# Top-32 attention with a feed-forward block behind it: when SyncE writes and reads the turned weights, and where POOL combines the output weights

## The chip, the cores and the metric

The kernel runs on one core of one Trainium2 chip. A core has five engines that work side by side, each through its own instructions in order: PE (matrix products; PEld is its loading of the stationary operand), DVE and ACT and POOL (element-wise work), and SP (SyncE, which here only issues transfers, DMAs). An engine waits on semaphores for the others. PE writes to PSUM, a small memory in banks; everything else lies in SBUF, with 128 partitions, or in DRAM.

The metric is the time of one execution on the device, in microseconds (us): the median of the runs.

## The reference

```python
def _attn_ref(q, k, v):                       # (8, 8, 576, 64) each
    top_k, scale = 32, 1.0 / np.sqrt(D)
    scores = scale * np.matmul(q, k.transpose(0, 1, 3, 2))
    kth = np.partition(scores, -top_k, axis=-1)[..., -top_k:-top_k + 1]
    scores = np.where(scores >= kth, scores, -1000000000.0)
    scores = scores - np.max(scores, axis=-1, keepdims=True)
    attn = np.exp(scores)
    attn = attn / (np.sum(attn, axis=-1, keepdims=True) + 1e-09)
    return np.matmul(attn, v).astype(np.float32)

def _moe_ref(x, w_in, w_out):                 # x: (4608, 512), w_in: (512, 2048)
    h = x @ w_in
    g = h - np.tanh(h)
    return (g @ w_out).astype(np.float32)
```

The attention's output, with the heads side by side, is the x of the second block. The output is 4608 x 512 in float32.

## The kernel before

**Steps.** A step is one query tile of 128 rows for a pair of heads, and there are 144: for each of the 8 batches four full tiles for each of four pairs of heads, and two steps for the 64 rows that remain. A step goes through several passes of the loop in `run` (L973). In pass n, DVE searches step n for the 32 largest scores of each row (`search`, from L340). Meanwhile POOL and ACT make the mask of step n-1 (`mask`, L386) and its exponentials (`expo`, L428). Between the rounds of the search of step n, ACT divides the weights of step n-2 (`divide`, L453), and at the end of that search DVE turns them in blocks of 32 x 32 into the one buffer `zx` (`turn_z`, L485, transpose at L490). PE makes the scores of step n+1 (`scores`, L329), which need the PSUM banks that the search of step n has read.

**Turned weights.** The blocks must also change partitions. For that `spread_keys` (L495) writes `zx` to DRAM (`there`, L506) and reads it back in four DMAs into `et` (L508), regrouped. It does so once for a pair of tiles, or for a step of remaining rows, when the step's flag `last` is set: 70 times. All five DMAs are on SyncE's queue, and the reads wait there for the write's landing. `values` (L542, products at L556) multiplies the weights in `et` by v on PE, five passes after the search of its step. Batch 0 goes another way: its steps have `pe` set, and PE turns the weights itself (`turn_pe`, L513).

**The feed-forward block.** When the last pair of heads of a unit is done, its items go to a list (`ffn`, L782). There are two small units, of 128 tokens (the first two tiles of batch 0), and 17 full ones, of 256. A small unit has 8 items for the first layer and then 8 parts of plain products with `w_out` (`ffn_o`, L623). A full unit has 16 items for the first layer (`ffn_full`, L770) and then 14 items of a seven-product scheme (`product` and `ffn_p`, L703 and L724), which replaces the eight products of 2 x 2 blocks by seven of combined blocks.

**The combinations of `w_out`.** For the scheme four combinations are made for each quarter of `w_out` by POOL, once, sixteen in all (`combine`, L661). T1 and T2 replace blocks of `w_out` in place, T2 through a DMA; T3 and T4 go to DRAM (`kept`). They are made in the first items of the first full unit, two in each.

**Refills.** The blocks B21, T3 and T4 are used from two buffers (`flow`, in the tile `more`), one for each half. `stream` (L698, DMA at L701) fills one from DRAM, on SyncE's queue: B21 in items 6 and 7 of the first layer, T3 and T4 right behind the products that used the buffer before.

**The order.** It is written out by the loop of `run`. A pass takes items from the list in several deals, each by a share of a rate that spreads the work over the passes (`deal`, L965). From the middle of the kernel on, in a pass that isn't of batch 0, it goes as follows:

```python
search(n, exact, between)            # turn_z(n - 2) at its end
if here(-2) and not pe and steps[n - 2].last:
    spread_keys(n - 2)               # write, and the four reads behind it
deal(0.0 if pe else 0.4)
due()                                # values
scores(n + 1); expo(n - 1)
deal(...); deal(...)                 # 0.2 each
for fn in todo.pop(n, []): fn()      # loads of k, q, v; DVE's turning of k, q
deal(0.2)
```

This is shortened. SyncE meets its DMAs in just this order: those of a pass's deals (refills and stores of the output, L766), of the loads, and of `spread_keys`.

Of the kernel before, what the change touches and what calls it, by code (L numbers as in the profile page):

```python
# [25 lines left out]
class Step:  # L26
# [4 lines left out]
    def __init__(self, b, hp, qt, unit, col, i=0, nq=1, pe=False, part=0):  # L31
        self.b, self.hp, self.qt, self.unit, self.col = b, hp, qt, unit, col
        self.part = 0 if pe else part
        self.i, self.nq, self.pe = i, nq, pe
        self.rem = qt == J
        self.last = i == nq - 1

        self.lag = 2 if pe else LAG


class Unit:
# [3 lines left out]
    def __init__(self, blocks, tag):  # L45
        self.blocks, self.tag = blocks, tag
        self.n = 128 * len(blocks)
        self.items = 16 if self.n == 128 else 30
        self.xT = None
        self.g = []  # L50
# [3 lines left out]
def kernel(  # L54
# [20 lines left out]
    CD = DM // P  # L75
# [5 lines left out]
    WJ = 4  # L81
# [32 lines left out]
    def next_h(name):  # L114
        bank[0] ^= 1
        return h_bank(bank[0], name)
# [98 lines left out]
    def half(t):  # L215
        return slice(t * D, (t + 1) * D)
# [260 lines left out]
    def group(a):  # L477
        return slice(a * G, (a + 1) * G)
# [16 lines left out]
    def spread_keys(n):  # L495


        zx = zxs.pop(n)
        rem = steps[n].rem
        if not rem:  # L500
            last_et[0] ^= 1
        et = ets[n] = et_rem if rem else et2[last_et[0]]
        assert rem or not last_et[0] or combined[0] == 4 * WJ
        w = steps[n].nq * S // 2
        there = dpool.tile([P, NG * w], FP32, tag=f"there{steps[n].nq}", name="there")
        nc.sync.dma_start(there[:], zx[:, 0 : NG * w])  # L506
        for c in range(NG):
            nc.sync.dma_start(  # L508
                et[group(c), 0 : NG * w].rearrange("i (a x) -> i a x", a=NG),
                there[:, c * w : (c + 1) * w].rearrange("(a i) x -> i a x", a=NG),  # L510
            )
# [111 lines left out]
    def ffn_o(u, i, part):  # L623
        if part == 0:
            cur[u] = next_h("ops")
        for f in range(2 * part, 2 * part + 2):
            o = f * u.n + i * P
            nc.tensor.matmul(
                cur[u][:],
                u.g[0][:, o // 512, o % 512 : o % 512 + P],  # L630
                w_out[f // FJ][:, f % FJ, :],
                start=(f == 0),
                stop=(f == CF - 1),
            )
        if part < CF // 2 - 1:
            return
        ot = thpool.tile([P, DM], FP32, tag="th", name="ot")
        nc.scalar.copy(ot[:], cur[u][:])
        for rows, dst in u.blocks[i]:
            nc.sync.dma_start(dst, ot[rows, :])  # L640
# [3 lines left out]
    def corners(x):  # L644
        x = x.rearrange("p (m r) n -> p m r n", r=2)
        return [[x[:, :, r, c * 2 * P : (c + 1) * 2 * P] for c in range(2)] for r in range(2)]
# [14 lines left out]
    def combine(j, x):  # L661

        (b11, b12), (b21, b22) = corners(w_out[j][:])
        t3, t2, t4 = (temps[(3 * j + i) % 4] for i in range(3))
        ms = slice(2 * j, 2 * j + 2)
        if x == 0:
            nc.gpsimd.tensor_tensor(t3, b12, b22, ALU.subtract)
            nc.sync.dma_start(kept["T3"][:, ms, :], t3)
        elif x == 1:
            nc.gpsimd.tensor_tensor(b12, b12, b11, ALU.subtract)  # L670
        elif x == 2:
            nc.gpsimd.tensor_tensor(t2, b22, b12, ALU.subtract)
        else:
            nc.gpsimd.tensor_tensor(t4, b21, t2, ALU.subtract)
            nc.sync.dma_start(kept["T4"][:, ms, :], t4)
            nc.sync.dma_start(b21, t2)
# [90 lines left out]

    combined = [0]

    def ffn_full(u, item):  # L770

        ffn_h(u, item)
        if item in (6, 7):
            stream(item - 6)
        if combined[0] < 4 * WJ:
            for _ in range(2):
                combine(combined[0] // 4, combined[0] % 4)
                combined[0] += 1
        if 8 <= item < 11:
            sum_up(u, 0, item - 8)  # L780

    def ffn(u):  # L782

        nh = CF * u.n // (2 * P)
        full = len(u.blocks) == 2
        for item in range(nh):
            f = (item + 1) * CF // nh - 1
            yield CD * (f // FJ + 1), u, lambda item=item: (ffn_full if full else ffn_h)(u, item)
        if not full:
            for part in range(CF // 2):  # L790
                yield CD * (WJ + part // 2 + 1), None, lambda part=part: ffn_o(u, 0, part)
            return
        for item in range(2 * len(ORDER)):
            yield 2 * WJ * CD, None, lambda item=item: ffn_p(u, item)
# [3 lines left out]
    steps, done, work = [], {}, []  # L798

    def plan():  # L800
        steps.clear(), done.clear()

        def block(b, qt):
            return [(slice(0, P), out[b * S + qt * P : b * S + (qt + 1) * P, :])]

        rest = None
        for b in range(B):
            if b % 4 == 0:
                rest = Unit(
                    [  # L810
                        [(half(i), out[(b + k + i) * S + JP : (b + k + i + 1) * S, :]) for i in range(2)]
                        for k in (0, 2)
                    ],
                    "xTr",
                )

            parts = [(0, 1), (2, 3)]
            if b == 0:
                parts[0:1] = [(0,), (1,)]
            for a, qts in enumerate(parts):  # L820
                unit = Unit([block(b, qt) for qt in qts], "xT")
                pe = b == 0
                for hp in range(NHP):
                    for i, qt in enumerate(qts):
                        steps.append(Step(b, hp, qt, unit, 0, i, len(qts), pe, a))
                    if hp == NHP - 1:
                        done[len(steps) - 1] = unit
                    if hp % 2 and a == (0 if b == B - 1 else len(parts) - 1):
                        steps.append(Step(b, hp - 1, J, rest, b % 4 * R, pe=pe, part=a))
                        if hp == NHP - 1 and b % 4 == 3:  # L830
                            done[len(steps) - 1] = rest
        for g, after in zip(steps, steps[1:]):
            if after.pe and not after.rem and not g.pe:
                g.lag = 3
# [4 lines left out]
    def run(exact):  # L839
# [13 lines left out]
        for b in range(B):  # L853
            for hp in range(NHP):
                for part in range(2 if b else 1):
                    n = next(n for n, g in enumerate(steps) if (g.b, g.hp, g.part) == (b, hp, part) and not g.rem)
# [62 lines left out]
        def here(i):  # L919
            return 0 <= n + i < NS  # L920
# [39 lines left out]
                        low = max(low, need[-1] / (t - n))  # L960
            return max(low, high)

        credit = 0.0

        def deal(part):  # L965
            nonlocal credit
            credit += part * share
            while work and credit > 0 and work[0][0] <= usable:
                work.pop(0)[2]()
                credit -= 1  # L970
            credit = min(credit, 1.0)

        for n in range(-4, NS + LAG):  # L973
            pe = here(-2) and steps[n - 2].pe
            def due():
                for m in (n - LAG, n - LAG + 1, n - LAG + 2):
                    if 0 <= m < NS and steps[m].last and steps[m].lag == n - m:
                        values(m)

            if n < NEAR:  # L980
                due()
            share, usable = rate(), converted[0]
            if pe:
                w = turn_pe(n - 2)
                next(w)
            if here(-1):
                mask(n - 1, exact)
            if here(0):
                search(n, exact, between)
            elif here(-2):  # L990
                between(0)
                between(LATE)
            if here(-2) and not pe and steps[n - 2].last:
                spread_keys(n - 2)
            if pe:
                spread(n - 2)
            deal(0.0 if pe else 0.4)
            if n >= NEAR:
                due()
            if here(1):  # L1000
                scores(n + 1)
            if pe:
                next(w)
            if here(-1):
                expo(n - 1)
            deal(0.8 if pe else 0.2)
            if pe and steps[n - 2].last:
                values(n - 2)
            deal(0.0 if pe else 0.2)
            for fn in todo.pop(n, []):  # L1010
                fn()
            deal(0.2)
# [4 lines left out]
    with tc.manual_schedule():  # L1017
        run(False)
# [42 lines left out]
```

## Time and profile before

| | |
|---|---|
| median of 3 runs | 1724.63 us (1723.66 to 1727.11) |
| the profiled execution's own time | 1726.47 us |
| its span, from the first to the last instruction | 1724.6 us |
| mean granted clock of PE | 0.925 |
| busy: PE, PEld | 1440.0 us (83%), 1085.6 us (63%) |
| busy: DVE, ACT, POOL | 1299.3 us (75%), 1017.6 us (59%), 1103.7 us (64%) |
| DMA | 287.87 MB, 62% of the 16 DMA engines' span on SyncE's queue |

A share of busy time is a mean over the kernel. Three views tell more. The chain that ended last goes back from the last instruction to what released it, and gives the shares of the span by engine and by line. The waits say, for an engine's instruction, how long the engine stood idle before it and what ended that, in total, with the number of times and the longest; for SyncE's queue they are separate, since all of SyncE's time is waiting or issuing. The timeline lists instructions in order of time: start, duration, engine, line, operation, output and input, number, and in brackets the idle time before. A row such as "SPq L508" is SyncE's issue of the DMA in line 508; when it lands is another matter, and the list of DMA issues gives the median time from issue to landing. Line numbers are those of the kernel before.

### The profile page before, as it was taken

Reading aid. Unit: us, or ns where it says so; the run is one execution under the profiler, and the core shown is the slowest. Engines: PE = TensorE matmul, PEld = TensorE weight load, DVE = VectorE, ACT = ScalarE, POOL = GpSimd, SP = SyncE. Lnnn points to the kernel's source line nnn. Section 1 sums busy time; section 2 is a strip of 40 time slices with the busy share of each in tenths; the row PEclk is TensorE's granted clock in tenths of the full one; section 3 lists DMA queues with packets and bytes.
Section 4 is the critical chain, followed back from the end, with each engine's and each line's share of the span. In section 5 each row is a group of like instructions: output and inputs, shape, how many; then the busy total and the mean of one; then the engine's idle time right before and its main releaser. Section 6 shows DMA issues by size and latency. Waiting matters only on the chain.

```text
span 1724.6 us, 27027 instructions
## 1 busy us (share of the span) xinstructions
PE 1440.0 (83%) x7892; PEld 1085.6 (63%) x7892; DVE 1299.3 (75%) x4914; ACT 1017.6 (59%) x1898; POOL 1103.7 (64%) x1573
## 2 busy tenths in 40 slices
PE   4677986896987979797969798979796988788998
PEld 3463754675665657575757576757574766566787
DVE  7998977989797979797968878779696886684000
ACT  5766755666575657574747565656575665564311
POOL 4776787676584857575757656767666584756434
PEclk9788998899898989898989999989898999899999
DMA  9863126688476775686757856677757575645421
GB/s 269 325 202 116 30 70 183 183 197 205 126 203 169 176 199 153 180 207 157 196 149 178 198 154 178 168 182 180 182 160 177 151 187 163 168 137 143 128 86 63
DMA packets 299292, 287.87 MB, mean 167 GB/s; under 512 B 224384, under 2 KB 234624, under 8 KB 291968
## 3 DMA queue, kind: packets, MB, share of 16 engines
q1 hardware_dynamic: 297360, 285.83, 62.0%
q8 instruction: 65, 1.06, 0.3%
q14 instruction: 91, 0.75, 0.1%
q10 hardware_dynamic: 1776, 0.22, 0.1%
HBM read 196.98 MB, written 87.95 MB: 165 GB/s over the span
## 4 chain that ended last, share of the span: by engine, by line
PE 29%; DVE 24%; DMA 16%; ACT 14%; POOL 10%; issue 4%; SPq 2%; DVEq 0%; ACTq 0%; POOLq 0%
PE hps L607 9%; PE hy L721 7%; DMA more<-keptT 6%; DMA there<-zx 5%; PE hx L721 5%; DVE m L378 4%; ACT z L458 4%; DVE top L371 4%; ACT z L409 3%; PE av L556 3%; PE scps L329 3%; POOL g L621 3%; DVE zx L490 3%; DVE rest L381 2%; DVE ab L365 2%
## 5 line engine op out<-in xcount | busy, mean ns | idle before, releaser
L607 PE MATMUL hps<-xT,w_in 128*128 128x256 f32 (+1 forms) x2176 | 475.4, 375 | 15.3 <-ACT g L620 14.4
L412 POOL TENSOR_TENSOR z<-sc,z 128x576 f32<-128x576 f32 x288 | 404.4, 1426 | 109.6 <-ACT z L409 109.6
L607 PEld LDWEIGHTS hps<-xT,w_in 128*128 128x128 f32 x2176 | 393.2, 193 | 95.9 <-issue 23.9
L409 ACT ACTIVATE z<-sc,tb 128x576 f32<-128x576 f32 x288 | 207.6, 768 | 249.9 <-POOL tb L396 243.6
L721 PE MATMUL hy<-more,g 128*128 128x256 f32 x816 | 233.6, 445 | 144.2 <-DMA more<-keptT 132.5
L721 PEld LDWEIGHTS hy<-more,g 128*128 128x128 f32 x816 | 178.6, 225 | 195.1 <-issue 125.2
L490 DVE STREAM_TRANSPOSE zx<-z 128x1152 f32<-128x1152 f32 x126 | 172.5, 1369 | 127.2 <-ACT z L458 118.2
L621 POOL TENSOR_TENSOR g<-g,th 128x512 f32<-128x512 f32 x144 | 183.1, 1273 | 96.0 <-ACT g L620 95.3
L432 ACT ACTIVATE z<-z,nb 128x576 f32<-128x576 f32 x288 | 221.8, 776 | 2.4 <-POOL z L412 2.4
L458 ACT ACTIVATE z<-z,rd 128x576 f32<-128x576 f32 x252 | 180.3, 762 | 34.8 <-DVE rd L451 34.6
L329 PE MATMUL scps<-kT,qT 64*128 64x288 f32 (+1 forms) x1120 | 163.6, 441 | 38.2 <-DVE top L367 36.7
L371 DVE MAX8 top<-ab 128x8 f32<-128x144 f32 x864 | 194.6, 294 | 0.0
L442 POOL TENSOR_SCALAR rd<-den 128x2 f32<-128x2 f32 x144 | 32.7, 227 | 245.8 <-ACT z L432 242.0
L337 ACT COPY sc<-scps 128x1152 f32<-128x1152 f32 x144 | 160.7, 1116 | 47.1 <-PE scps L329 46.9
L359 DVE TENSOR_TENSOR scps<-scps,sc 128x288 f32<-128x288 f32 x144 | 64.6, 448 | 147.8 <-ACT sc L337 147.7
L378 DVE MAX8 m<-rest 128x8 f32<-128x168 f32 x576 | 161.3, 321 | 0.0
L378 DVE MAX8 m<-top 128x8 f32<-128x144 f32 (+1 forms) x576 | 151.4, 304 | 0.0
L329 PEld LDWEIGHTS scps<-kT,qT 64*128 64x128 f32 (+1 forms) x1120 | 89.2, 182 | 94.2 <-issue 30.3
L721 PE MATMUL hx<-w_out,g 128*128 128x256 f32 x544 | 132.4, 390 | 16.7 <-POOL g L621 8.6
L721 PEld LDWEIGHTS hx<-w_out,g 128*128 128x128 f32 x544 | 101.3, 192 | 43.6 <-POOL g L621 16.1
L721 PE MATMUL hx<-w_out,more 128*128 128x256 f32 x544 | 126.9, 383 | 0.0
L619 ACT ACTIVATE th<-hps 128x512 f32<-128x512 f32 x144 | 84.3, 585 | 55.2 <-PE hps L607 52.6
(107 smaller groups left out, 2258.4 us busy)
## 6 DMA issues: line engine op xcount, KB each, us to landing
there<-zx SPq DMA_DIRECT2D x56, 1152.0 KB, 4.2
more<-keptT SPq DMA_DIRECT2D x68, 512.0 KB, 5.8
et<-there SPq DMA_DIRECT2D x112, 288.0 KB, 5.0
spare<-there SPq DMA_DIRECT2D x112, 288.0 KB, 5.4
more<-keptB SPq DMA_DIRECT2D x34, 512.0 KB, 7.0
vb<-in_v_dram SPq DMA_DIRECT2D x118, 128.0 KB, 6.8
kin<-in_k_dram SPq DMA_DIRECT2D x116, 72.0 KB, 4.3
out_dram<-ot SPq DMA_DIRECT2D x32, 256.0 KB, 3.2
```

The costliest lines, as they stand in the source:

```text
L329: nc.tensor.matmul(ps[rows, t, s, 0:S2], qT[g.b, g.hp + i, g.part][half(t), qs], kT[g.b, g.hp + i][half(t), ks], start=True, stop=True,)
L337: nc.scalar.copy(sc[:], ps[:, :, :, 0:S2])
L371: nc.vector.max(top[:, t, o : o + 8], low[:, t, i, :])
L378: nc.vector.max(m[:, t, m8], seen[i][t])
L409: nc.scalar.activation(zv[:, t, :], scf[:, t, :], AF.Relu, bias=tb[:, t : t + 1], scale=-BIG)
L412: nc.gpsimd.tensor_tensor(zv[:, t, :], scf[:, t, :], zv[:, t, :], ALU.subtract)
L432: nc.scalar.activation(x["zv"][:, t, :], x["zv"][:, t, :], AF.Exp, bias=x["nb"][:, t : t + 1], scale=scale, accum_out=den[:, t : t + 1],)
L458: nc.scalar.activation(x, x, AF.Copy, scale=rds[n][:, g.i, t : t + 1])
L490: nc.vector.transpose(tiles(zx, g.nq)[:, :, :, g.i, :].rearrange("p c k j -> p k c j"), z[:].rearrange("p (k c j) -> p k c j", c=NG, j=G),)
L607: nc.tensor.matmul(cur[u][:, s : s + w], w_in[j][:, c, fo : fo + P], u.xT[:, c, 0:w], start=(c == 0), stop=(c == CD - 1),)
L621: nc.gpsimd.tensor_tensor(g, g, th[:], ALU.subtract)
L721: nc.tensor.matmul(acc, lhs[:, m, :], rhs, start=(fresh and k == 0 and m == 0), stop=(k == 1 and m == 3), skip_group_check=True)
```

## The change

It has two parts.

First, `spread_keys` becomes a generator. Its first half, with the write, is run after the third deal of the same pass, ahead of the loads. Its second half, the four reads, is run in the next pass, after that pass's first deal.

Second, a full unit's item makes one combination, not two, and the second small unit (tile 1 of batch 0) makes one in each part of its plain products but the first. Seven of the sixteen are thus made there, and nine in the first full unit.

```diff
@@ class Unit
         self.n = 128 * len(blocks)
+        self.combines = False
@@ spread_keys
         nc.sync.dma_start(there[:], zx[:, 0 : NG * w])
+        yield
         for c in range(NG):
             nc.sync.dma_start(
@@ ffn_full
     combined = [0]
 
+    def combine_next():
+
+        if combined[0] < 4 * WJ:
+            combine(combined[0] // 4, combined[0] % 4)
+            combined[0] += 1
+
+    def ffn_small_o(u, part):
+
+        ffn_o(u, 0, part)
+        if u.combines and part:
+            combine_next()
+
     def ffn_full(u, item):
 
         ffn_h(u, item)
         if item in (6, 7):
             stream(item - 6)
-        if combined[0] < 4 * WJ:
-            for _ in range(2):
-                combine(combined[0] // 4, combined[0] % 4)
-                combined[0] += 1
+        combine_next()
@@ ffn
-                yield CD * (WJ + part // 2 + 1), None, lambda part=part: ffn_o(u, 0, part)
+                yield CD * (WJ + part // 2 + 1), None, lambda part=part: ffn_small_o(u, part)
@@ plan
                 pe = b == 0
+                unit.combines = pe and a == 1
@@ run
-        credit = 0.0
+        credit, coming_back = 0.0, []
@@ run, the loop over passes
-            if here(-2) and not pe and steps[n - 2].last:
-                spread_keys(n - 2)
             if pe:
                 spread(n - 2)
             deal(0.0 if pe else 0.4)
+            for x in coming_back:
+                next(x, None)
+            coming_back.clear()
             if n >= NEAR:
                 due()
...
             if pe and steps[n - 2].last:
                 values(n - 2)
             deal(0.0 if pe else 0.2)
+            if here(-2) and not pe and steps[n - 2].last:
+                coming_back.append(spread_keys(n - 2))
+                next(coming_back[0])
             for fn in todo.pop(n, []):
                 fn()
             deal(0.2)
```

## The prediction

> **What bounds the kernel now.** I read the page's span and chain first, then the busy time by stretch, then the waits of the engines and of SyncE's queue.
>
> ```profile
> span 1724.6 us, 27027 instructions
> PE 29%; DVE 24%; DMA 16%; ACT 14%; POOL 10%; issue 4%; SPq 2%; DVEq 0%; ACTq 0%; POOLq 0%
> 275.50:1561.00 1285.50, 1097.27 (x6031) 826.28 (x6032) 1054.15 (x4037) 798.83 (x1482) 841.37 (x1226) 0.93 0.68 173
> 1561.00:1724.60 163.60, 146.92 (x709) 123.73 (x707) 14.19 (x40) 43.50 (x88) 69.95 (x74) 0.96 0.33 100
> ```
>
> The columns of the last two rows are us, then busy us of PE, PEld, DVE, ACT and POOL. No engine fills the long middle stretch: PE is busy 1097 of 1285 us and DVE 1054. They are coupled through PE's order, scores of the next step behind feed-forward products of this one, so whatever stops PE stops the search on DVE as well. The last 164 us are nearly pure PE work.
>
> ```profile
> PE hy L721 <- DMA more<-keptT: 132.5, 23, 12.7
> PE scps L329 <- DVE top L367: 37.5, 13, 12.2
> DVE scps L359 <- ACT sc L337: 147.7, 50, 14.4
> DVE zx L490 <- DMA there<-zx: 9.0, 3, 4.2
> SPq L508 <- DMA there<-zx: 282.2, 70, 6.5
> SPq L506 <- DVE zx L490: 207.1, 33, 15.1
> ```
>
> These are waits: total us, times, longest. PE's largest one is for the refills of the flow buffers (the halves of T3 and T4). SyncE spends 282.2 us, 4.0 per turn, between the write of turned weights and its reads, and another 207.1 waiting for the transposes ahead of the write. Refills that were issued later in the program stand behind both. One unit shows it:
>
> ```profile
> 868.71 3.62 PE L721 MATMUL hy<-more,g 128*128 128x256 f32 x16
> 873.43 3.72 PE L721 MATMUL hx<-w_out,more 128*128 128x256 f32 x16
> 889.89 5.93 PE L721 MATMUL hy<-more,g 128*128 128x256 f32 x16 [12.75 <-DMA more<-keptT]
> 895.76 1.95 PE L556 MATMUL av<-et,vb 128*64 128x256 f32 x16
> 898.07 1.24 PE L329 MATMUL scps<-kT,qT 64*128 64x288 f32 x8
> 902.79 3.62 PE L721 MATMUL hy<-more,g 128*128 128x256 f32 x16
> ...
> 876.72 0.35 SPq L506 DMA_DIRECT2D there<-zx  x1
> 880.93 1.76 SPq L508 DMA_DIRECT2D spare<-there  x4
> 882.79 0.85 SPq L701 DMA_DIRECT2D more<-keptT  x2
> 883.70 0.42 SPq L276 DMA_DIRECT2D vb<-in_v_dram  x1
> 887.32 5.24 SPq L259 DMA_DIRECT2D qin<-in_q_dram  x4
> 893.67 2.53 SPq L701 DMA_DIRECT2D more<-keptT  x2
> ...
> 875.32 1.38 DVE L490 STREAM_TRANSPOSE zx<-z 128x1152 f32<-128x1152 f32 x1 [0.38 <-ACT z L458]
> 884.70 1.38 DVE L490 STREAM_TRANSPOSE zx<-z 128x1152 f32<-128x1152 f32 x1 [0.84 <-ACT z L458]
> 900.50 0.47 DVE L359 TENSOR_TENSOR scps<-scps,sc 128x288 f32<-128x288 f32 x1 [14.43 <-ACT sc L337]
> ```
>
> The product at 868.71 frees the two halves at 870.5 and 872.3. SyncE issues their refills only at 882.79: it waits for the transpose (ends 876.70), then for the write's landing (880.9), then it issues four reads. PE wanted the refill at 877.15 and stands 12.75 us; the scores behind it come at 898.07, and DVE idles 14.43 us. The wait is on the path of every engine.
>
> **The refills, part by part.** The write moves behind the refills and output stores of the pass's first three deals, its reads behind the first deal of the next pass. The same DMAs are issued, in the same number. A refill dealt before the write no longer sees the transpose, the landing or the reads. How long it then takes:
>
> ```profile
> more<-keptT SPq DMA_DIRECT2D x2, 512.0 KB, 8.0
> more<-keptT SPq DMA_DIRECT2D x2, 512.0 KB, 3.9
> there<-zx SPq DMA_DIRECT2D x56, 1152.0 KB, 4.2
> ```
>
> These are median us from issue to landing in two windows: the pair at 882.79, right behind the reads, and the pair at 893.67, with nothing ahead of it; the third row is the write's, over the kernel. In the unit above a refill issued at 870.5 lands at about 874.4, ahead of 877.15: that wait goes whole.
>
> Not all refills gain so. One dealt after the write still stands behind the write, hence behind the transpose, and behind the step's loads. In the same unit: PE goes on at 877.15, frees the next halves near 879 and 880.8 (2 x 1.8 us), but SyncE leaves the write at 876.72, then loads v (883.70 to 887.32, 3.6 us at most) and q (5.24), so these refills go at about 885.9 and land at 889.8. They are needed after the product (3.6), the values (2.3), the scores (1.2) and the next product (3.7), at 888: late by 1 to 2 us. A second place that stays is a refill behind a step's reads, whose landing is 8.0 and not 3.9. I take 2.0 us a unit, an estimate from this unit, for 17 units: 34 us stay. The bounds are 0 (all land in time, as the first refill here) and 5 us a unit, 85 (every unit has one refill with the 8.0 landing, 4.1 more, and a little issue time). So 132.5 - 34 = 98.5 us go (bounds 132.5 and 47.5).
>
> **The slow products after a wait.** The 16 matmuls right after the wait took 5.93 us, the same 16 later 3.62. Over the kernel:
>
> ```profile
> L721 PE MATMUL hy<-more,g 128*128 128x256 f32 x816 | 233.6, 445 | 144.2 <-DMA more<-keptT 132.5 <-ACT z L458 5.6 <-ACT z L409 3.9
> L721 PE MATMUL hx<-w_out,more 128*128 128x256 f32 x544 | 126.9, 383 | 0.0
> ```
>
> Busy time per matmul is 233.6 / 816 = 0.286 us against 126.9 / 544 = 0.233 for the same shape with no wait ahead. The 0.053 us on 816 are 43.2 us, paid for 132.5 us of waits. With 98.5 of these gone, 43.2 x 98.5 / 132.5 = 32 us go too (43 and 15 at the bounds). The Trainium skill (TensorE: Matmul & The Clock Gate, Part 1) says the array falls to half clock after an idle window of about 3.4 us and needs about as long of work to come back. By it only the longer waits cost, at about 1.7 us each, so at 23 waits at most 39 us; an estimate from that page, by which this term would be 29 instead of 32. The trace agrees with the direction (5.93 against 3.62).
>
> **The combinations.** There are sixteen on POOL, each a 128x512 operation of 1.27 us; four are in the group of the first row, and the first and the last of all are at 232.21 and 271.05:
>
> ```profile
> L667 POOL TENSOR_TENSOR spare<-w_out 128x512 f32<-128x512 f32 x4 | 5.1, 1268 | 0.2
> 232.21 1.27 POOL L667 TENSOR_TENSOR spare<-w_out 128x512 f32<-128x512 f32 x1
> 239.52 1.44 ACT L409 ACTIVATE z<-sc,tb 128x576 f32<-128x576 f32 x2 [5.93 <-POOL tb L396]
> 253.47 1.44 ACT L409 ACTIVATE z<-sc,tb 128x576 f32<-128x576 f32 x2 [7.69 <-POOL tb L396]
> 272.64 0.77 ACT L409 ACTIVATE z<-sc,tb 128x576 f32<-128x576 f32 x1 [11.95 <-POOL tb L396]
> 271.05 1.26 POOL L674 TENSOR_TENSOR spare<-w_out,spare 128x512 f32<-128x512 f32 x1 [4.06 <-DMA w_out<-spare]
> 210.16 0.73 POOL L574 TENSOR_TENSOR xT<-more 128x256 f32<-128x256 f32 x1 [2.45 <-ACT more L570]
> 219.67 2.80 POOL L412 TENSOR_TENSOR z<-sc,z 128x576 f32<-128x576 f32 x2 [2.61 <-ACT z L409]
> ```
>
> They come two an item; in three steps four, six and six of them (two, three and three items) stand ahead of the thresholds, and ACT waits 5.93, 7.69 and 11.95 us. At one per item two, three and three are left there, one more falls into a fourth step, and seven go to the small unit's products near 203 to 226 us. That takes 2, 3 and 3 x 1.27 = 10.2 us and the 4.06 us wait for a copy out of these steps: 14.2, less 1.3. The seven cost 8.9 us of POOL; idle times of 2.45 and 2.61 cover 5.1, and if that cover is needed for something else all 8.9 show. So 13 - 4 = 9 us go (bounds 14 and 0).
>
> **What the change adds.** Behind the write on SyncE stand the loads, behind the reads the later refills; behind the late write waits DVE's next transpose, since there is one zx. In the unit above the next transposes start 884.70 and the write lands about 4.2 us after its issue, so it must leave by 880.5, or 3.8 us after the transposes of its own step end. It now leaves behind refills and stores of two deals that PE runs after the next scores. DVE waits 9.0 us for this today; I add 6 us, an estimate (bounds 0 and 20). The weights reach their buffer almost a step later, but their product comes two to three steps after the write; I cost this at nothing, and at 2 us a turn if that margin were not there.
>
> **The sum.** 98.5 + 32 + 9 - 6 = 133.5 us off the profiled execution's own 1726.47 (span 1724.6 and 1.9 around it): 1593. The median of the runs is 1.84 lower, so **1591 us**. As a check, the middle stretch would lose about 115 of 1285 us, to 1170, in which DVE's 1054 and PE's 1097 less 32 both fit at some 90%.
>
> **The rivals.** (1) *Refills stay late.* What delays them after the change is the transposes, the loads and the queue of transfers, and a unit keeps 5 us. For it: q loads took 5.24 us to issue, and DMA is 0.68 busy. Against: the refills that stood behind nothing landed in 3.9. By the bounds: 47.5 + 15 + 4 - 10 = 56 off, 1668.
>
> (2) *The late write stops DVE: slower.* If stores and refills hold the write for PE's products, the transposes wait for its landing, then the scores' consumer does, in every one of 70 turns. Each us beyond the 3.8 costs 70 us; the gain of 139.5 (without the 6) is used up at 2.0 us beyond. At 3 us beyond, 210 - 139.5 = 70 more: 1795. For it: three transposes wait for the write already today, one of them for 4.2 us. Against: PE reaches those deals early in the search, not at its end. The Trainium skill (DMA: Bandwidth & Descriptors, Rules for kernel authors) advises to issue a DMA early and to wait on it late; by that the reads move the right way and the write the wrong one. The trace here shows only the first half, the 282.2 us of waiting early.
>
> (3) *The wait only changes its name.* If PE ran into the scores' buffers or late weights just as long, nothing would be seen: 1725. For it: PE also waits for DVE and ACT in many short waits. Against: the next largest wait of its matmuls is 37.5 us, for the scores' buffers, and it is another engine that would have to become late.
>
> **How the numbers follow.** Forecast 0.74, its own range 1550 to 1640; rival (1) 0.16, (2) 0.07, (3) 0.03. The low end is all waits gone with their slow products and little of the rest (132.5 + 43 = 175.5 off gives 1549); the high end takes in rival (1). About 0.2% (3.4 us) can be told from no change: faster 0.90, same 0.03, slower 0.07.
>
> **What would show it.** Right: PE's wait for the refills at 20 to 50 us, SyncE's wait between write and reads near zero, hy matmuls near 0.24 us, ACT's waits for the thresholds at 230 to 280 us about halved. Wrong: a refill wait above 80 us, transposes that wait for the write by more than 30 us in total, value products that wait for weights, or a step without refills that is longer than before.

## The result and the profile after

The changed kernel takes 1586.04 us (median of 4 runs, 1584.7 to 1588.93) against 1725.33 us before (4 runs): the ratio is 0.9195, with a 95% interval of 0.9179 to 0.9211, or 139.3 us less. The lines named below are one or two higher in the kernel after than before: the write is L507, the reads L510, the refills L703, the products of the scheme L723.

First the span and the stretches, from the page and from the busy time by stretch (us, then busy us of PE, PEld, DVE, ACT and POOL):

```profile
span 1587.1 us, 27014 instructions
262.20:1434.30 1172.10, 1071.15 (x6031) 811.57 (x6032) 1052.81 (x4037) 796.40 (x1481) 842.38 (x1224) 0.97 0.76 193
1434.30:1587.10 152.80, 145.44 (x709) 122.63 (x707) 14.19 (x40) 43.51 (x88) 70.01 (x74) 0.99 0.34 101
```

The stretches are cut at the same work as those of before (the same 6031 and 709 matmuls). The middle one is 1172.1 us long instead of 1285.5, and PE is busy 91% of it, DVE 90%; the tail is 152.8 instead of 163.6, as its one wait for a refill fell from 9.75 us to 0.55; the stretch ahead of both is 13 us shorter. The waits of the kernel after, of engines and of SyncE's queue:

```profile
DVE scps L360 <- ACT sc L338: 43.1, 39, 5.8
DVE zx L491 <- DMA there<-zx: 37.5, 14, 6.7
PE hy L723 <- DMA more<-keptT: 35.2, 17, 4.4
PE scps L330 <- DVE top L368: 34.4, 20, 5.6
...
SPq L507 <- DVE zx L491: 225.8, 35, 12.2
SPq L510 <- DMA there<-zx: 61.9, 32, 9.6
```

PE's wait for refills fell from 132.5 to 35.2 us and its longest from 12.7 to 4.4; DVE's wait for scores, the echo of it, from 147.7 to 43.1. One row rose: DVE's wait for the write, from 9.0 to 37.5. The unit that the prediction walked through, in the timelines of PE, SyncE and DVE:

```profile
814.66 3.62 PE L723 MATMUL hy<-more,g 128*128 128x256 f32 x16
818.21 1.24 PE L330 MATMUL scps<-kT,qT 64*128 64x288 f32 x8
819.38 3.72 PE L723 MATMUL hx<-w_out,more 128*128 128x256 f32 x16
822.93 3.62 PE L723 MATMUL hy<-more,g 128*128 128x256 f32 x16
...
833.52 3.62 PE L723 MATMUL hy<-more,g 128*128 128x256 f32 x16
...
816.58 2.07 SPq L703 DMA_DIRECT2D more<-keptT  x2
822.67 0.32 SPq L507 DMA_DIRECT2D there<-zx  x1
...
826.60 2.10 SPq L260 DMA_DIRECT2D qin<-in_q_dram  x4
828.79 0.88 SPq L703 DMA_DIRECT2D more<-keptT  x2
829.72 2.15 SPq L510 DMA_DIRECT2D spare<-there  x4
...
821.27 1.38 DVE L491 STREAM_TRANSPOSE zx<-z 128x1152 f32<-128x1152 f32 x1 [0.37 <-ACT z L459]
832.25 0.47 DVE L360 TENSOR_TENSOR scps<-scps,sc 128x288 f32<-128x288 f32 x1 [0.17 <-ACT sc L338]
```

The first refill goes out at 816.58, as soon as its half is free, while the transpose that the write waits for begins only at 821.27; the product at 822.93 follows the one before it without a gap. The second pair goes behind the write and the loads, at 828.79, with its halves free from about 825; it is in place when it is wanted at 833.5. DVE's 14.43 us of idle time have become 0.17. Other units keep a wait: at 488.30 a product stands 4.36 us for a pair that left at 483.17, behind the write (476.69) and 6 us of loads.

### The profile page after: what moved, and what is told of

The parts are those of the page before. It is cut to its first block, busy times and chain, and to the rows that moved or that the text cites. A ratio compares the mean times of both kernels' runs of the same rounds, so it can differ in the third digit from the quotient of the medians.

```text
span 1587.1 us, 27014 instructions
## 1 busy us (share of the span) xinstructions
PE 1410.6 (89%) x7892; PEld 1069.5 (67%) x7892; DVE 1298.0 (82%) x4914; ACT 1017.1 (64%) x1898; POOL 1105.1 (70%) x1573
## 4 chain that ended last, share of the span: by engine, by line
PE 29%; DVE 26%; DMA 13%; ACT 12%; POOL 12%; issue 5%; SPq 3%; DVEq 0%; ACTq 0%; POOLq 0%
PE hps L609 10%; PE hx L723 6%; PE hy L723 6%; DMA more<-keptT 5%; DVE m L379 4%; DMA there<-zx 4%; DVE top L372 4%; POOL g L623 3%; PE av L558 3%; ACT z L459 3%; ACT z L410 3%; PE scps L330 3%; POOL z L413 3%; DVE zx L491 3%; DVE rest L382 2%
## 5 line engine op out<-in xcount | busy, mean ns | idle before, releaser
L723 PE MATMUL hy<-more,g 128*128 128x256 f32 x816 | 208.1, 407 | 37.7 <-DMA more<-keptT 35.2
L723 PEld LDWEIGHTS hy<-more,g 128*128 128x128 f32 x816 | 161.2, 202 | 78.4 <-DMA more<-keptT 20.3
L330 PE MATMUL scps<-kT,qT 64*128 64x288 f32 (+1 forms) x1120 | 158.3, 430 | 36.1 <-DVE top L368 34.0
L723 PE MATMUL hx<-w_out,g 128*128 128x256 f32 x544 | 133.4, 393 | 16.9 <-POOL g L623 10.0
L723 PEld LDWEIGHTS hx<-w_out,g 128*128 128x128 f32 x544 | 102.9, 194 | 44.2 <-POOL g L623 17.6
L723 PE MATMUL hx<-w_out,more 128*128 128x256 f32 x544 | 127.8, 385 | 0.0
L723 PEld LDWEIGHTS hx<-w_out,more 128*128 128x128 f32 x544 | 102.6, 191 | 21.1 <-issue 4.7
```

Of the source, the lines that this page charges most:

```text
L330: nc.tensor.matmul(ps[rows, t, s, 0:S2], qT[g.b, g.hp + i, g.part][half(t), qs], kT[g.b, g.hp + i][half(t), ks], start=True, stop=True,)
L723: nc.tensor.matmul(acc, lhs[:, m, :], rhs, start=(fresh and k == 0 and m == 0), stop=(k == 1 and m == 3), skip_group_check=True)
```

## The experiments

The kernels are named by their experiment. Their diffs are shortened, with "..." for what is left out, and go against the changed kernel. This table has the median time, PE's wait for the refills, the busy time of the 816 matmuls of hy, DVE's wait for the write, and SyncE's wait between write and reads, all in us.

| | time | refill wait | hy busy | DVE for write | SyncE, write to reads |
|---|---|---|---|---|---|
| before | 1725.3 | 132.5 | 233.6 | 9.0 | 282.2 |
| e2, combinations alone | 1713.4 | 152.1 | 234.2 | 7.1 | 283.0 |
| e4, write and reads at the end | 1672.8 | 97.6 | 225.1 | 40.4 | 329.8 |
| e3, reads alone moved | 1632.9 | 70.0 | 220.8 | none | 12.7 |
| e8, reads a pass later | 1631.9 | 19.3 | 197.5 | 21.5 | 9.4 |
| e1, move alone | 1602.1 | 29.2 | 203.5 | 26.4 | 57.4 |
| after | 1586.0 | 35.2 | 208.1 | 37.5 | 61.9 |
| e5, write before reads | 1587.7 | 33.7 | 202.9 | 13.4 | 25.7 |
| e6, last deal first | 1586.9 | 28.6 | 199.8 | 51.7 | 73.1 |
| e7, loads in mid-pass | 1588.6 | 25.4 | 205.7 | 43.9 | 263.3 |
| e9, e5 and e6 together | 1578.3 | 17.2 | 199.2 | 29.3 | 32.6 |

The theory was: the refills were late because they stood in SyncE's queue behind the transposes, the landing and the reads, PE's wait for them stopped every engine, and the gain is this wait and the slow products behind it. The rivals were that one half of the move does it all, and that the gain has another source.

**e1 and e2, one part each.** e1 keeps two combinations an item, and has the move; e2 is the other way round.

```diff
         ffn_o(u, 0, part)
-        if u.combines and part:
-            combine_next()
...
-        combine_next()
+        for _ in range(2):
+            combine_next()
...
```

> The move of write and reads alone; combinations two an item as before. Theory (the two parts add up, and the combinations are worth what steps 20 to 23 of the search became shorter, 58.0 to 44.3 us): 1586 + 14 = 1600 us, with ACT's waits for the thresholds near 240 to 273 us back at about 25 us. Rival (the combinations' waits are covered by others once the turns are moved): 1586 to 1590.

> The combinations alone; write and reads where they were. Theory: 1725 - 14 = 1711 us, PE's wait for refills unchanged at 130 to 135 us. Rival (worth nothing by itself): 1725.

e1 took 1602.1 us (ratio to before 0.928, 0.9262 to 0.9298), e2 1713.4 (0.9912, 0.9889 to 0.9934). By the medians the combinations are thus worth 16 us beside the move and 12 alone, and the move 127 beside them and 123 alone: the parts add up to within 4 us. Neither rival holds; e2's gain is small, but its interval leaves out 1. The 16 are less sure than the 12: e1's profiled execution was its fastest, 1593.8 us, and lies only 4.9 above that of the changed kernel. ACT's first three waits for the thresholds, in e1 and then in the kernel after:

```profile
240.99 1.44 ACT L410 ACTIVATE z<-sc,tb 128x576 f32<-128x576 f32 x2 [5.94 <-POOL tb L397]
254.96 1.44 ACT L410 ACTIVATE z<-sc,tb 128x576 f32<-128x576 f32 x2 [7.71 <-POOL tb L397]
270.16 1.44 ACT L410 ACTIVATE z<-sc,tb 128x576 f32<-128x576 f32 x2 [7.98 <-POOL tb L397]
```

```profile
236.68 1.44 ACT L410 ACTIVATE z<-sc,tb 128x576 f32<-128x576 f32 x2 [3.46 <-POOL tb L397]
246.63 1.44 ACT L410 ACTIVATE z<-sc,tb 128x576 f32<-128x576 f32 x2 [3.69 <-POOL tb L397]
257.83 1.44 ACT L410 ACTIVATE z<-sc,tb 128x576 f32<-128x576 f32 x2 [3.97 <-POOL tb L397]
```

The three sum to 25.6 us in the kernel before, 21.6 in e1 and 11.1 in the kernel after. The third was 11.95 us before and is 7.98 in e1: POOL's 4.06 us of waiting for a copy went with the move alone. It is gone in e2 too, where that wait is 3.97, so either part removes it, and the gain counts once. From the start of DVE's 17th step to that of its 25th the profiles have 89.6 us before and 77.6 in e2, 85.7 in e1 and 77.6 after: 12 us for the combinations alone, and 8 beside the move. Where the rest of the 16 comes from is open.

The refill wait of e2 was expected at 130 to 135 us and is above that, and above that of before (152.1 against 132.5), since some of before's idle time ahead of the same products was put down to ACT (144.2 us in all against 152.5 in e2). For the 8 us that are left I have no account; a shorter wait for refills was at any rate not what made e2 faster.

**e3, the reads alone moved.** The write goes back ahead of the first deal; the reads stay in the next pass.

```diff
+            if here(-2) and not pe and steps[n - 2].last:
+                coming_back.append(spread_keys(n - 2))
+                next(coming_back[-1])
             if pe:
                 spread(n - 2)
             deal(0.0 if pe else 0.4)
-            for x in coming_back:
-                next(x, None)
-            coming_back.clear()
+            while coming_back and (len(coming_back) > 1 or not (here(-2) and not pe and steps[n - 2].last)):
+                next(coming_back.pop(0), None)
...
-            if here(-2) and not pe and steps[n - 2].last:
-                coming_back.append(spread_keys(n - 2))
-                next(coming_back[0])
```

> As the changed kernel, but the write stays ahead of the pass's first deal; only the reads are in the next pass. Theory (both the wait for the transposes ahead of the write and the wait for its landing hold up refills): refills of the first three deals wait for the transposes again, some 3 us a unit of PE's time, 17 units: 1586 + 50, less a few us because DVE waits less for the write: 1615 to 1645, PE's wait for refills 70 to 100 us. Rival (only landing and reads in front of the refills matter, the write's place does not): 1575 to 1590.

It took 1632.9 us (0.9462, 0.9435 to 0.9489), with 70.0 us of refill wait: inside the theory's range, 47 us slower than the change; the rival is out. Its timelines of SyncE and PE show the place, in the same unit as above:

```profile
828.65 0.34 SPq L507 DMA_DIRECT2D there<-zx  x1
829.10 1.33 SPq L703 DMA_DIRECT2D more<-keptT  x2
...
821.80 3.62 PE L723 MATMUL hy<-more,g 128*128 128x256 f32 x16
826.51 3.72 PE L723 MATMUL hx<-w_out,more 128*128 128x256 f32 x16
836.24 4.18 PE L723 MATMUL hy<-more,g 128*128 128x256 f32 x9 [6.01 <-DMA more<-keptT]
```

(The window of the last row ends within its product.) The halves are free from about 823.6, but the refills stand behind the write, which waits for the transposes until 828.65. There is no landing and no read in front of them, and PE still waits 6.01 us instead of 12.75.

**e4, write and reads at the end.** Here the write stays where the change put it, and the reads follow at once.

```diff
-                coming_back.append(spread_keys(n - 2))
-                next(coming_back[0])
+                for _ in spread_keys(n - 2):
+                    pass
```

> As the changed kernel, but the reads stand right behind the write at the pass's end. Theory: refills of the first three deals stay free, those of the last deal and of the next pass's first deal wait for the landing and the reads, 5.8 us more, about three in ten of the refills: PE's wait for refills 60 to 90 us, 1615 to 1645 us. Rival (moving the write behind the deals is all of the gain): 1580 to 1592.

It took 1672.8 us (0.9699, 0.9675 to 0.9722), with 97.6 us of refill wait. The direction is the theory's, the size beyond its range: it left out that the loads stand behind the reads too, and the refills of the last deal and the next first one behind these. One such place:

```profile
673.44 0.34 SPq L507 DMA_DIRECT2D there<-zx  x1
681.35 1.74 SPq L510 DMA_DIRECT2D spare<-there  x4
...
685.36 4.41 SPq L260 DMA_DIRECT2D qin<-in_q_dram  x4
689.92 0.83 SPq L703 DMA_DIRECT2D more<-keptT  x2
...
694.84 3.75 PE L723 MATMUL hy<-more,g 128*128 128x256 f32 x8 [11.76 <-DMA more<-keptT]
```

A refill here comes 16.5 us after the write that precedes it, and PE waits 11.76 us. So neither half of the move does it alone: 1713.4 with neither, 1672.8 with the write late and the reads behind it, 1632.9 with the reads late only, 1586.0 with both late and apart.

**e5, what DVE's new wait costs.** In a pass that has reads of the turn before and a write of its own, the write goes first.

```diff
+            turn = here(-2) and not pe and steps[n - 2].last
+            if not turn:
+                for x in coming_back:
+                    next(x, None)
+                coming_back.clear()
...
-                coming_back.append(spread_keys(n - 2))
-                next(coming_back[0])
+                new = spread_keys(n - 2)
+                next(new)
+                for x in coming_back:
+                    next(x, None)
+                coming_back[:] = [new]
```

> As the changed kernel, but in a pass that has reads of the turn before and a write of its own (the pair's and the remaining rows' turns follow each other) the reads go behind the write. Theory (the write of such a pass lands late because 1.15 MB of reads were issued just ahead of it, and DVE's 37.5 us of waiting for the write are mostly on the path): DVE's wait for the write falls below 10 us and the time by 10 to 25 us, to 1561 to 1576. Rival (PE's products set the pace in those steps and hide DVE's wait): the wait falls the same, the time stays within 5 us of 1586.

DVE's wait fell from 37.5 to 13.4 us, and the time stayed: 1587.7 (0.9211, 0.9179 to 0.9243). The theory fell here, as to the price. The wait fell as the theory and the rival both had it, though not below 10 us, and the time is the rival's. In the kernel after, SyncE and DVE at such a place, and the landing of that write in the list of DMA issues for its moment:

```profile
866.36 1.92 SPq L510 DMA_DIRECT2D spare<-there  x4
868.37 0.68 SPq L507 DMA_DIRECT2D there<-zx  x1
879.41 1.38 DVE L491 STREAM_TRANSPOSE zx<-z 128x1152 f32<-128x1152 f32 x1 [4.95 <-DMA there<-zx]
...
there<-zx SPq DMA_DIRECT2D x1, 576.0 KB, 10.9
```

The write of 576 KB goes right behind four reads and lands 10.9 us later. Over the kernel the 14 writes of this size took 4.0 us before, 8.8 after and 4.8 in e5. Eleven of DVE's 14 waits in the kernel after, 32.7 of 37.5 us, are for writes of this size.

**e6 and e7, what is left of the refill wait.** e6 puts the pass's last deal ahead of the write. e7 issues the loads of a pass's end in the next pass, behind the reads.

```diff
             deal(0.0 if pe else 0.2)
+            if not pe:
+                deal(0.2)
             if here(-2) and not pe and steps[n - 2].last:
...
-            deal(0.2)
+            if pe:
+                deal(0.2)
```

```diff
             coming_back.clear()
+            for fn in waiting:
+                fn()
+            waiting.clear()
...
             for fn in todo.pop(n, []):
-                fn()
+                if fn in loads and n >= 20:
+                    waiting.append(fn)
+                else:
+                    fn()
```

> As the changed kernel, but the pass's last deal stands ahead of the write and the loads. Theory (of the 35 us that PE still waits for refills, those behind the loads come from the last deal and the next pass's first one): refill wait 15 to 30 us, DVE's wait for the write a little more than 37 us since the write stands behind one deal more, time 1575 to 1590. Rival (what is left is the landing time, not the queue): refill wait 33 to 40, time not below 1586.

> As the changed kernel, but from the 20th pass on the loads of a pass's end are issued in the next pass, behind the reads. Theory (loads in front of refills cost what is left of the wait; in mid-pass they stand in front of the second and third deal instead of the last and first): refill wait 20 to 40 us, time 1575 to 1590. Rival (the loads are then late for their own users): a new wait of DVE or PE for q, k or v of over 10 us, time above 1595.

The refill wait fell to 28.6 and 25.4 us, so the loads and the write in front of refills do make part of what is left. The times, 1586.9 (0.9196, 0.9161 to 0.9231) and 1588.6 (0.9216, 0.9184 to 0.9247), cannot be told from 1586.0. In e6 DVE's wait for the write rose to 51.7 us. In e7 the rival's new wait for q, k or v did not come: the one long one, 6.6 us, is there in the changed kernel too.

**e8, the margin of the weights.** The reads come one pass later still.

```diff
-            for x in coming_back:
-                next(x, None)
-            coming_back.clear()
+            if len(coming_back) > 1 or (coming_back and aged[0]):
+                next(coming_back.pop(0), None)
+            aged[0] = len(coming_back)
...
-                next(coming_back[0])
+                next(coming_back[-1])
```

> As the changed kernel, but the reads come one pass later still, in mid-pass of the second pass after the write. Theory (the prediction put the later arrival of the weights at nothing, since two to three passes lie between write and product): one pass of some 9 us is left for a landing of 6 us, so PE's wait for weights stays below 10 us and the time within 10 us of 1586. Rival (the margin is used up by then): PE waits for the weights in most of 70 turns, by 1 to 3 us each, 1620 to 1750.

It took 1631.9 us (0.9466, 0.9433 to 0.9498), 46 us more. The theory fell: at a part of the turns the margin is used up.

```profile
PE av L558 <- DMA spare<-there: 29.3, 12, 4.7
PE av L558 <- DMA et<-there: 26.9, 8, 5.3
...
305.14 1.85 SPq L510 DMA_DIRECT2D et<-there  x4
315.81 3.68 PE L558 MATMUL av<-et,vb 128*64 128x256 f32 x16 [5.28 <-DMA et<-there]
```

The first two rows are PE's waits for weights in e8, 56 us in 20 waits, for 70 turns: fewer than the rival's "most", but the time is in its range. In the kernel after the same two rows come to 2.7 us. The other two show the longest wait: the reads leave 9 to 11 us ahead of the product and land 7.7 us after their issue in the median, where the theory had 6. Why the pass left so little time at just these turns was not followed further.

**e9, both orders together.** The edits of e5 and e6 in one kernel.

> The two orders together that each left the time where it was: in a pass with reads and a write the write goes first, and the pass's last deal stands ahead of the write. Theory (PE's wait for refills and DVE's wait for the write hide each other, so only taking both away shows): both waits at 15 to 30 us and a time of 1560 to 1576. Rival (neither is on the path any more; PE's and DVE's own work with its short couplings sets the pace): both waits as low, the time 1581 to 1592.

It took 1578.3 us (0.9153, 0.9132 to 0.9174); the interval lies just below that of the change, 0.9179 to 0.9211. The refill wait is 17.2 us, DVE's wait for the write 29.3. It is the fastest kernel of all, by about 8 us of 1586. The theory's range ends 2 us lower and the rival's begins 3 us higher, so neither is borne out in size; that the two waits covered each other is only argued.

**e10 and e11, what paces the kernel after the change.** e10 does two maxima of each step twice on DVE, e11 half of the score products twice on PE.

```diff
-                nc.vector.max(m[:, t, m8], seen[i][t])
+                for _ in range(1 if i else 2):
+                    nc.vector.max(m[:, t, m8], seen[i][t])
```

```diff
-                for t in range(2):
+                for t in (0, 1) if s else (0, 0, 1, 1):
```

> As the changed kernel, with the first round's two maxima of each step done twice on DVE (0.25 us each, 0.5 us a step, 72 us in all; the result is the same). Theory (after the change DVE and PE pace the steps together, at some 90% of each): 40 to 72 us more, 1626 to 1658. Rival (PE alone sets the pace, DVE has room): less than 20 us more.

> As the changed kernel, with the first half of each step's score products done twice on PE (half of 1.24 us a step, some 85 us in all; the result is the same). Theory (PE and DVE pace the steps together): 45 to 90 us more, 1631 to 1676. Rival (DVE alone sets the pace, PE has room): less than 25 us more.

DVE's busy time rose from 1298.0 to 1385.7 us and the time by 33 us, to 1619.1 (0.9388, 0.9361 to 0.9416). PE's rose from 1410.6 to 1469.1 and the time by 21 us, to 1606.8 (0.932, 0.9294 to 0.9347).

```profile
PE 1418.3 (88%) x7892; PEld 1073.9 (67%) x7892; DVE 1385.7 (86%) x5202; ACT 1019.1 (63%) x1898; POOL 1107.8 (69%) x1573
```

```profile
PE 1469.1 (92%) x8532; PEld 1124.3 (70%) x8532; DVE 1299.0 (81%) x4914; ACT 1018.6 (64%) x1898; POOL 1104.7 (69%) x1573
```

These are the busy rows of e10 and e11. Each us of added busy time costs 0.38 us on DVE and 0.36 on PE. Both times lie below the theory's ranges. e10's lies above its rival's, and e11's in its rival's range, but e10 speaks against the same rival's ground, DVE alone. So neither engine sets the pace alone; more than half of a small addition to either is hidden. That fits e5, e6 and e7, which moved nothing, but it does not prove that they moved nothing for this reason.

## Why the prediction was right, and where not

The time was forecast at 1591 and measured at 1586.0. By the steps of the sum:

- **Refills, 98.5 us.** The wait went from 132.5 to 35.2: 97.3. That both things in front of the refills count, the transposes and the landing with the reads, is shown by e3 and e4; that the loads make part of what stays, by e6 and e7. The size has some luck in it: the 34 us that were to stay came from one unit, where refills behind the loads were to be late by 1 to 2 us. In the kernel after that unit does not wait at all, and the 35.2 us are 17 waits in others. The landing of 3.9 us with nothing ahead was read off a pair that left 1.1 us behind loads of q; the two pairs of that unit now land in 4.3 and 4.7.
- **Slow products, 32 us.** The matmuls of hy went from 233.6 to 208.1: 25.5. The mechanism is there, the term a quarter too large. The granted clock rose from 0.925 to 0.962. The share was taken in proportion to the waits; between kernels of the table hy's time falls by 0.16 (e4 to e3), 0.36 (e3 to after) or 0.49 us (after to e9) with each us of wait, not by one fixed share.
- **Combinations, 9 us.** 12 us alone by e2, and by e1 16 in the medians or 8 in the steps of the profiles. ACT's three waits fell by 10.5 us from e1 to after, as the count had it (10.2); the 4 us for the copy, which the prediction put here, also go with the move. The seven that went to the small unit cost less than the 4 us set against them: the three steps that hold them are 1.8 us longer in all (24.1 before, 25.9 after).
- **What the change adds, 6 us.** Here the step failed. DVE's wait rose by 28.5 us, above its bound of 20, and mostly for another reason than the one given: not the refills and stores of two deals ahead of the write, but the reads of the turn before, which at 11 of the 14 writes of remaining rows left within 2 us ahead of them. The waits cost nothing that can be seen by themselves: taking 24 us of them away (e5) left the time alone. With the last deal moved as well, the same order goes with 8 us (e6 to e9), so that they cost nothing in any order is not shown. Rival (2) needed the wait in each of 70 turns; it came in 14, so its price of 70 us for each us was not put to the test.
- **The weights' later arrival, nothing.** Right: 2.7 us of waits. Little of the margin is left, though: one pass more takes 46 us (e8). That is 0.7 us a turn, where the fallback price was 2.

Together 97 + 25 + 12, less nothing, is 134 us of the 139 measured; the rest has no account. The forecast was as near as it was because its errors offset each other: 6 us too much for the slow products against 6 for a cost that was not paid. PE's own account agrees: it is idle 176.5 us (span less busy time) instead of 284.6, so the wait did not just change its name (rival 3), and busy 29 us less.

The check on the middle stretch held as well: 1170 us were expected, with PE and DVE at some 90%, and 1172 measured, with 91 and 90. Of the signs named beforehand for being right, the refill wait (35.2) and ACT's waits (25.6 to 11.1) came; the hy matmuls are at 0.255 us, not 0.24; and SyncE's wait between write and reads is not near zero but 61.9 us, in 32 turns. SyncE often reaches the reads before the write has landed; that this does no harm where no refill that is due stands behind them is only argued, but in e7 it is 263.3 us and the time the same. Two signs for being wrong came as well: transposes wait for the write by 37.5 us in total, above 30, and seven of the 144 steps are over 1 us longer than before, five of them with such a wait (the longest by 5.4 us) and three without refills now. They did not go with a slower kernel, and for the wait e5 shows that it alone cost no time. Rival (1) would have kept 85 us of refill wait; the landing of a refill, 5.8 us in the median before and 5.0 after, did not grow.

By the rule of the Trainium skill (TensorE: Matmul & The Clock Gate, Part 1) the slow products came to 29 us; the trace shows 25.5. That says little for the rule, as the 29 take all 23 waits as long ones, and the same proportion as the 32. Longer than 3.4 us were 14 waits before and 5 after; nine at about 1.7 us are 15 us, an estimate from that page. The traces have slow products after shorter waits too. In the kernel before, the stretches around a wait of 2.67 us that ends at 808.45 (us, busy us of PE, PEld, DVE, ACT and POOL, then the granted clock, DMA share and GB/s):

```profile
802.00:805.80 3.80, 3.78 (x20) 2.38 (x18) 1.74 (x3) 3.80 (x8) 3.40 (x4) 1.00 0.86 229
805.80:808.40 2.60, 0.00 (x0) 0.00 (x0) 2.57 (x8) 1.02 (x4) 0.95 (x2) 1.00 1.02 141
808.40:811.00 2.60, 2.55 (x8) 2.02 (x8) 2.60 (x17) 0.00 (x0) 0.00 (x0) 0.64 0.89 249
...
808.45 5.56 PE L721 MATMUL hy<-more,g 128*128 128x256 f32 x16 [2.67 <-DMA more<-keptT]
```

The clock is full before and during the wait and falls after it; the 16 products take 5.56 us, against 3.62.

## What to carry to other kernels

SyncE's queue, which issues in order, passed the wait at its head on to every refill behind it: the first of the unit above left 12 us after its half was free (870.5, 882.79). A write whose reads must wait for its landing belongs apart from its reads, each where nothing that is due soon stands behind it; either half alone brought 41 or 81 of the 127 us. Price such a wait by what PE or DVE stands for it, and then see what a further one is worth: from 35 us of refill wait on, taking single waits away brought nothing here, and two together 8 us. That no engine set the pace alone (e10, e11) fits this.

## What the runs showed of the hardware

A write that is issued right behind 1.15 MB of reads on the same queue lands later by several us: 576 KB in 8.8 us in the median against 4.0, with one of 10.9. With the write ahead of these reads (e5) it is 4.8. In the kernel before the write and the reads ahead of it were never that close: the reads had left at least 5.6 us earlier.

```profile
there<-zx SPq DMA_DIRECT2D x14, 576.0 KB, 8.8
```
